# Fused adaLN attention and MLP block: V projected in eight tiles and shifted by DMA, K's last heads in the padding, head loads on one queue, a new instruction order

## The chip, the core and the metric

The kernel runs on one core of one Trainium2 chip. The core has five engines that each run a list of their own in order: TensorE (PE in the profile; PEld is its weight load), VectorE (DVE), ScalarE (ACT), GpSimd (POOL) and SyncE (SP); the lists meet at semaphores. DMAs are issued from SP's or ACT's list and are moved by 16 DMA engines. The metric is the time of one execution on the device in microseconds (us), lower is better.

## The reference

One transformer block for 2048 tokens of width 448, all in bf16: a vector c makes six modulation vectors; then a sliding, dilated attention (16 heads of 28, each token sees itself and 7 earlier tokens at stride 2) and an MLP of width 1792, each behind a modulated layer norm and added back through a gate.

```python
mod = (silu(c) @ w_mod).reshape(1, 6, 1, -1)
sa, ca, ga, sb, cb, gb = (mod[:, i] for i in range(6))
h = layernorm(x) * (1 + ca) + sa
...
idx = pos[:, None] - (arange(8) * 2)[None, :]          # keys of a token, masked where < 0
attn = softmax(where(mask, einsum('bhsd,bhswd->bhsw', q, k[idx]) * 28 ** -0.5, -1e9))
o = einsum('bhsw,bhswd->bhsd', attn, v[idx])
...
x = x + ga * (o @ wo)
h = layernorm(x) * (1 + cb) + sb
x = x + gb * (silu(h @ w1) @ w2)
```

## The kernel before

**Tokens.** The dilation of 2 splits the tokens by parity: even and odd tokens never meet, and in one parity (1024 steps) a token sees its last 8 steps. The projections run over NC = 4 chunks of 512 tokens (CP = 256 steps of both parities). Attention runs over NB = 9 blocks: a block takes 128 steps of keys and gives 112 or, for block 0, 128 queries (`q_of`, `nq_of`, lines 69 to 75); block b's keys begin at step 112 b.

**Norm.** `norm1` (line 595) normalises a chunk, transposes it (chunk 0 on PE, `on_pe`, line 520; the others by DMA transposes on SP, `on_dma`, line 545) and modulates it into `h1`, with the contraction of 448 split into three and a half tiles of 128. Since a block of keys reaches back over the chunk's edge, `h1` has 128 steps of room in front, and `halo` (line 611) copies 32, 64 or 96 steps of the chunk before into it.

**Projections.** `project` (line 615). Heads are padded from 28 to 32 rows (`pad`, line 562, into `wp` and `wp3`, whose columns 28 to 31 are zero), so that a matmul tile holds four heads: four tiles g = 0 to 3 a chunk, each of which makes Q and K of four heads with N = 512 columns (two halves of 256 in chunk 0). Each tile is a `duo` (line 569): 14 matmuls of 64 rows, run in pairs on the two halves of the array, in a first part of 6 and a second of 8, with a `turn` on POOL between them (line 308: a nop that orders the two halves' exchange of PSUM banks). An eviction on ACT or DVE follows (line 629). V is projected block by block (line 636): nine duos of 448 columns, one for each attention block, evicted into one of four buffers `vb` (line 640).

**Attention.** For a block and parity `logits` (line 655) makes 16 small matmuls into two PSUM banks, two exps on ACT (line 678), a mask product on DVE (line 704). `values` (line 716) makes 32 matmuls of probabilities and V (line 730), a normalisation on DVE (lines 735, 736) and a DMA transpose into `oT` (line 740). `out_proj` (line 746) takes 256 tokens: 14 matmuls with `wo`, which was multiplied by its gate on DVE (line 879) and copied half by half between partitions by two DMAs on SP (lines 882, 883), then two adds on DVE (line 768).

**MLP.** `ffn1` (line 782): norm, transposes on SP, 7 duos of 512 columns, silu on ACT (line 794). `ffn2` (line 799): 28 matmuls for 256 tokens, an add (line 823), a store on SP (line 826). The last 256 tokens go in two plain accumulations (line 832), then an add and a store each (lines 838, 841).

**Order.** Nothing here is scheduled at run time. Each operation is a numbered `P.op`, and `ORDER` (line 44) is the written list of all numbers; `emit` (line 215) issues them in that order, each on its engine ("v" or "a" after a number chooses DVE or ACT where both can). So each engine has a fixed list, and an instruction that waits holds all behind it. PSUM has NPS = 4 pairs of banks; the probabilities have 5 buffers, V has 4. `warm_up` (line 403) runs WARM = 8 matmuls on zeroes, then JUNK = 5 pairs more where the order puts them.

**Loads.** x's first 256 tokens are loaded on SP and the next 256 (`x0b`) and c on ACT's queue; all other loads are on SP in the order's sequence: w_mod's first two vectors, `wqk`, the other chunks of x, `wv`, and so on (lines 378 to 400).

If a softmax sum is out of range, a flag makes the program run a slower, safe version of itself; it isn't taken here.

Of the kernel before, what the change touches and what calls it, by code (L numbers as in the profile page):

```python
# [11 lines left out]
ACTF = mybir.ActivationFunctionType  # L12
# [3 lines left out]
D = 448  # L16
# [19 lines left out]
HW = 128 + CP  # L36
WARM, JUNK = 8, 5
# [74 lines left out]
def dram(ap, row, col, dims):  # L112

    w = ap.ap[0][0]
    return bass.AP(ap.tensor, ap.offset + row * w + col, [[r * w + c, n] for r, c, n in dims])

# [125 lines left out]
def layer(ctx, tc, io, safe):  # L242
# [19 lines left out]
    NV, NP, NX, NO, NH, NB2 = (4, 5, 2, 2, 3, 2) if not safe else (3, 3, 2, 1, 3, 1)  # L262
# [5 lines left out]
    wqk_t = ct([128, 2 * KT * HW], "wqk")  # L268
    wqk = wqk_t[:, 0:6 * D].rearrange("p (k n) -> p k n", k=3)
    wv = ct([128, KT, D], "wv")  # L270
    wqk3 = ct([128, D], "wqk3")
    wp = ct([128, 3, 2 * H, 32], "wp")
    wp3 = ct([128, H, 32], "wp3")
    wo = ct([128, 2, KT, D], "wo")
    w1 = ct([128, 3, F], "w1")
    w13 = ct([128, F // 2], "w13")
    w2 = ct([128, NF, D], "w2")
# [40 lines left out]
    for r, n in (("ps", NPS), ("v", NV), ("p", NP), ("xn", NX), ("o", NB2), ("out", NO), ("dma", 8)):  # L318
        P.resource(r, n)
# [679 lines left out]
```

## Time and profile before

| | us |
|---|---|
| median of three runs | 172.31 (170.99, 172.31, 172.62) |
| the profiled execution | 171.64 |
| its span | 169.9 |
| busy: PE, ACT, DVE, POOL | 162.0, 114.5, 96.1, 33.2 |
| F1 matmuls (line 791), F2 (lines 808, 832) | 44.7, 39.9 and 5.5 |
| QK matmuls (line 627) | 13.4, 7.0 and 6.7 by shape |
| V matmuls (line 638), out-projection (line 753) | 11.3 and 3.3, 13.0 |
| exps (line 678), silus (line 794) | 31.5, 27.3 |
| table loads on ACT (line 321) | 10.3 (8) |

The span is what the trace covers, from the first to the last event on the core. Busy times of matmuls count from the start of one to its modelled end, so they run over each other where matmuls are pipelined; the time that one costs PE is its distance to the next. In the lines below, "idle before" is time that the engine stood still just ahead of the instruction, and the name behind the arrow is what ended it. "SPq" and "ACTq" are DMA issues of these engines.

### The profile page before, as it was taken

Reading aid. Unit: us, or ns where it says so; the run is one execution under the profiler, and the core shown is the slowest. Engines: PE = TensorE matmul, PEld = TensorE weight load, DVE = VectorE, ACT = ScalarE, POOL = GpSimd, SP = SyncE. Lnnn points to the kernel's source line nnn. Section 1 sums busy time; section 2 is a strip of 40 time slices with the busy share of each in tenths; the row PEclk is TensorE's granted clock in tenths of the full one; section 3 lists DMA queues with packets and bytes.
Section 4 is the critical chain, followed back from the end, with each engine's and each line's share of the span. In section 5 each row is a group of like instructions: output and inputs, shape, how many; then the busy total and the mean of one; then the engine's idle time right before and its main releaser. Section 6 shows DMA issues by size and latency. Waiting matters only on the chain.

```text
span 169.9 us, 4812 instructions
## 1 busy us (share of the span) xinstructions
PE 162.0 (95%) x2015; PEld 83.9 (49%) x2015; DVE 96.1 (57%) x189; ACT 114.5 (67%) x163; POOL 33.2 (20%) x88
## 2 busy tenths in 40 slices
PE   7799999899999999999999999999999999999990
PEld 2258644545554564455644544655544444445450
DVE  4777999899979963895352577732473000000451
ACT  3148999999876889999878998662767862420000
POOL 7342424730502221132000205120150000000000
PEclk9959999999999999999999999999999999999999
DMA  4994448489979874022020030086008000000031
GB/s 142 289 326 165 99 94 314 78 202 242 176 185 252 177 198 106 0 66 46 20 54 0 4 90 22 2 112 178 6 10 224 0 4 0 0 4 0 38 136 64
DMA packets 32054, 17.51 MB, mean 103 GB/s; under 512 B 23896, under 2 KB 31640, under 8 KB 32024
## 3 DMA queue, kind: packets, MB, share of 16 engines
q1 hardware_dynamic: 31872, 16.90, 39.9%
q8 instruction: 17, 0.28, 0.7%
q10 hardware_dynamic: 152, 0.23, 0.5%
q14 instruction: 13, 0.11, 0.2%
HBM read 9.12 MB, written 1.84 MB: 64 GB/s over the span
## 4 chain that ended last, share of the span: by engine, by line
PE 75%; ACT 10%; DMA 6%; issue 3%; DVE 2%; POOL 1%; ACTq 0%; POOLq 0%
PE ps L791 25%; PE ps L808 22%; PE ps L627 7%; PE ps L753 6%; PE ps L638 5%; ACT p L678 4%; PE ps L730 4%; DMA wqk<-in_A_wqkv_dram 3%; PE ps L832 3%; PE ps L670 3%; DMA x_all<-in_A_x_dram 2%; ACT h L536 2%; ACT qk L630 1%; POOL rs L487 1%; ACT both L480 1%
## 5 line engine op out<-in xcount | busy, mean ns | idle before, releaser
L791 PE MATMUL ps<-h,w 64*128 64x512 bf16 x392 | 44.7, 376 | 0.0
L808 PE MATMUL ps<-w,both 64*128 64x448 bf16 x392 | 39.9, 349 | 0.0
L794 ACT ACTIVATE both<-ps 128x1024 bf16<-128x1024 f32 x28 | 27.3, 1023 | 13.9 <-PE ps L791 13.8
L678 ACT ACTIVATE p<-ps 128x896 bf16<-128x896 f32 (+1 forms) x36 | 31.5, 928 | 3.3 <-PE ps L670 3.2
L791 PEld LDWEIGHTS <-w 64*128 64x128 bf16 x392 | 19.5, 94 | 21.6
L808 PEld LDWEIGHTS <-both 64*128 64x128 bf16 x392 | 18.9, 94 | 17.7
L823 DVE TENSOR_TENSOR ot<-ps,x_all 128x896 bf16<-128x896 f32 x7 | 7.6, 1088 | 34.6 <-PE ps L808 34.3
L627 PE MATMUL ps<-h,wp 64*128 64x256 bf16 (+1 forms) x224 | 20.4, 323 | 0.6 <-ACT h L536 0.4
L627 PEld LDWEIGHTS <-wp 64*128 64x128 bf16 x280 | 13.9, 94 | 11.3 <-issue 1.1
L704 DVE TENSOR_TENSOR p<-p,maskb 128x1792 bf16<-128x1792 bf16 (+1 forms) x18 | 19.3, 1098 | 0.0
L768 DVE SCALAR_TENSOR_TENSOR x_all<-ps,x_all 128x448 bf16<-128x448 f32 x16 | 9.3, 618 | 9.7 <-PE ps L753 9.7
L487 POOL TENSOR_TENSOR rs<-rs,negh 128x2 f32<-128x2 f32 x16 | 13.8, 861 | 1.3
L753 PE MATMUL ps<-wo,oT 64*128 64x448 bf16 x112 | 13.0, 350 | 0.0
L480 ACT ACTIVATE wqk<-x_all,mv 128x448 bf16<-128x448 bf16 x16 | 10.7, 667 | 3.2 <-POOL mv L477 3.0
L477 POOL TENSOR_SCALAR mv<-sums 128x2 f32<-128x2 f32 x10 | 4.8, 479 | 40.0 <-DVE x_all L768 22.2
L638 PE MATMUL ps<-wv,h 64*128 64x448 bf16 x98 | 11.3, 350 | 0.2
L557 DVE TENSOR_SCALAR h<-h,modc 128x512 bf16<-128x512 bf16 x19 | 6.8, 408 | 6.6 <-DMA h<-xn 6.6
L630 ACT CAST qk<-ps 128x1024 bf16<-128x1024 f32 (+1 forms) x12 | 10.0, 871 | 0.7 <-PE ps L627 0.7
L321 ACT ACT_TABLE_LOAD x8 | 10.3, 1283 | 0.1
L486 POOL TENSOR_SCALAR rs<-mv 128x2 f32<-128x2 f32 x10 | 3.6, 356 | 33.3 <-ACT wqk L480 14.5
L736 DVE TENSOR_TENSOR o<-ps,rc 112x896 bf16<-112x896 f32 (+1 forms) x9 | 9.8, 1091 | 0.4
L501 DVE TENSOR_SCALAR xn<-x_all,mv,rs 128x512 bf16<-128x512 bf16 x23 | 8.8, 406 | 1.7 <-POOL rs L487 1.7
(84 smaller groups left out, 161.8 us busy)
## 6 DMA issues: line engine op xcount, KB each, us to landing
out_dram<-ot SPq DMA_DIRECT2D x7, 224.0 KB, 2.2
both<-in_w_mod_dram SPq DMA_DIRECT2D x2, 672.0 KB, 6.0
x_all<-in_A_x_dram SPq DMA_DIRECT2D x3, 448.0 KB, 7.0
w<-in_B_w_dram SPq DMA_DIRECT2D x3, 448.0 KB, 4.2
w<-in_B_w_dram SPq DMA_DIRECT2D x1, 896.0 KB, 5.3
both<-in_w_mod_dram SPq DMA_DIRECT2D x2, 336.0 KB, 5.8
w<-in_B_w_dram SPq DMA_DIRECT2D x1, 672.0 KB, 5.4
wqk<-in_A_wqkv_dram SPq DMA_DIRECT2D x1, 448.0 KB, 5.7
```

The source lines that it names most:

```text
L321: P.load = lambda t: S.preload_act_table(ACTF.Exp if t == "e" else ACTF.Silu)
L480: S.activation(out=scratch[late], in_=x_all[:, us[j], :], func=ACTF.Square, bias=mv[:, j, 0:1], accum_out=mv[:, j, 1:2])
L487: G.tensor_tensor(out=rs[:, j:j + n], in0=rs[:, j:j + n], in1=negh[:, 0:n], op=ALU.pow)
L627: return T.matmul(ps[:, j, 0:2 * n], lhsT=w.rearrange("p h d -> p (h d)"), rhs=h[rows, :, t, c0:c0 + n], start=start, stop=stop)
L630: copy_on(o)(out=qk[:, :, g, :, s0:s0 + n], in_=ps[:, :, 0:2 * n].rearrange("p j (t s) -> p j t s", t=2))
L638: return T.matmul(ps[:, j, 0:D], lhsT=h[rows, j, t, b0:b0 + 128], rhs=wv[rows, t, :], start=start, stop=stop)
L678: S.activation(out=out_, in_=ps[:, :, 0:4 * nq].rearrange("p j (g q) -> p j g q", q=nq), func=ACTF.Exp, scale=SCALE)
L704: V.tensor_tensor(out=p, in0=p, in1=maskb[:, 1 if b == 0 else 0, 0:nq].unsqueeze(1).to_broadcast([128, H, nq]), op=ALU.mult)
L753: return T.matmul(box["ps"][:, j, 0:D], lhsT=oT[rows, j, kk, s0:s0 + 128], rhs=wo[rows, j, kk, :], start=start, stop=stop)
L791: return T.matmul(ps[:, j, :], lhsT=w, rhs=h[rows, :, t, :], start=start, stop=stop)
L794: S.activation(out=hid[:, k % 2, :, i, :], in_=ps[:], func=ACTF.Silu)
L808: return T.matmul(box["ps"][:, par, 0:D], lhsT=hid[rows, k % 2, f % 2, f // 2, 128 * (2 * i + par):128 * (2 * i + par) + 128], rhs=w2[rows ...
```

## The change

1. **V once in eight tiles.** V is projected for the eight aligned tiles of 128 steps, two a chunk, into three buffers `va`. Blocks 0 and 8 coincide with tiles 0 and 7. For each of blocks 1 to 7 two DMAs inside SBUF copy the two parts of their 128 steps from two neighbouring tiles into one of three buffers `vb`. The halos and `h1`'s room for them go.
2. **Q and K in seven tiles.** In chunks 2 and 3 K's last four heads are computed in the padding: 4 heads of 28 columns are 112 columns, and seven tiles have 4 spare columns for each of 4 heads. Nine small copies on POOL (`fill`) put these weights there, after QK of chunk 0 and ahead of QK of chunk 1, from `wp` and three more small loads (`wx`). The fourth tile then makes only Q, 256 columns to a PSUM bank. Four DMAs a chunk (`move`) bring K's rows from the padding of the seven tiles to their place; block 4's logits need chunk 2's, block 6's need chunk 3's.
3. **Loads of the head.** w_mod's first vectors are loaded from ACT's queue; c and x0b on SP, x0b behind `wqk`. Later weight loads, V copies, moves and stores may be on either queue, as the order says.
4. **Another order**, with JUNK = 7.

```diff
-WARM, JUNK = 8, 5
+WARM, JUNK = 8, 7
...
-    NV, NP, NX, NO, NH, NB2 = (4, 5, 2, 2, 3, 2) if not safe else (3, 3, 2, 1, 3, 1)
+    NA, NV, NP, NX, NO, NH, NB2 = (3, 3, 5, 2, 2, 3, 2) if not safe else (3, 3, 3, 2, 1, 3, 1)
...
+    ld_ma = load_mod(0, 2 * D, [], ("act",))
+    tab = P.op(("act", 1290.0), lambda o: S.preload_act_table(ACTF.Silu), [ld_ma[1]["deps"][0]], name="table")
...
+    ld_x[0].append(load(224, after=[x["deps"][0] for x in [ld_qk[0][0], ld_qk[1][0], ld_qk[3][0]]], **first_x(1), run=1792, name="x0b"))
...
+    def fill(out_, m0, in_, t0, t1, deps, name="fill"):
+
+        to = out_[:, m0:m0 + 4 * (t1 - t0), DH:32].rearrange("p (t r) c -> p t r c", r=4)
+        return P.op(("pool", 300.0), lambda o: G.tensor_copy(out=to, in_=spread(in_, t0, t1)), deps, name=name)
...
+    def move(r, s0, n, deps):
+
+        return sp(680.0, lambda o: queue(o).dma_start(out=qk[32 * r:32 * r + DH, 1, 3, :, s0:s0 + n], in_=qk_t[32 * r + DH:32 * r + 32, 0:7, :, s0:s0 + n]), list(deps), 1700.0,
+                  kb=28.0, run=512, eng=EITHER, name="mv")[0]
...
-            for g in range(4):
+            for g in range(4 if k < 2 else 3):
...
+            if k > 1:
+
+                def make(ps, j, kk, rows, t, start, stop, c0=c0):
+                    w = wq3[rows, kk // 3] if j and kk in (1, 3) else wp[rows, kk, 12:16, :] if kk < 3 else wp3[rows, 12:16, :]
+                    return T.matmul(ps[:, j, 0:n], lhsT=w.rearrange("p h d -> p (h d)"), rhs=h[rows, :, t, c0 + n // 2 * j:c0 + n // 2 * j + n // 2], start=start, stop=stop)
...
+                done = done + [move(r, s0, n, done) for r in range(4)]
...
+        for t in (2 * k, 2 * k + 1):
+            def make(ps, j, kk, rows, kt, start, stop, t=t):
+                return T.matmul(ps[:, j, 0:D], lhsT=h[rows, j, kt, 128 * (t % 2):128 * (t % 2) + 128], rhs=wv[rows, kt, :], start=start, stop=stop)
...
+            def shifted(o, b, up):
+                r = 16 * b
+                to, way = (slice(r, 128), slice(0, 128 - r)) if up else (slice(0, r), slice(128 - r, 128))
+                queue(o).dma_start(out=v_of[b]()[to], in_=va_of[b - 1 + int(up)][way])
```

The numbers of the orders say little by themselves; in names, PE's list from the first QK to the first out-projection is (a and b are the two parts of a duo, Lb.p the logits of block b and parity p, AV the product with V, WO the out-projection):

```
before: QK0 first half | QK0 second half with L0.0 inside | L0.1 | V0 | V1a L1.0 V1b | QK1 (L1.1 inside) | AV0 |
        gate of wo | AV1 | L2.0 | V2 V3a L2.1 V3b | QK2 two tiles (L3.0 inside) | AV2 | WO0.0a L3.1 WO0.0b | ...
after:  junk | QK0 first half | transposes of its second half | gate of w2 | L0.0 | QK0 second half | L0.1 | V0 |
        L1.0 | gate of wo | V1a L1.1 V1b | QK1 | AV0 | V2a L2.0 V2b | second modulation | AV1 | V3a L2.1 V3b |
        QK2 two tiles (L3.0 inside) | AV2 | QK2 third tile (L3.1 inside) | WO0.0a | half tile | V5 | WO0.0b ...
```

Other lists, after: on SP, V2's copy for block 2 stands behind a load of w1; then a DMA transpose of chunk 3, one of `oT`, the first copy of `wo`, a V copy for block 3, the second copy of `wo`. On DVE the product of `wo` and its gate stands behind chunk 2's modulation and block 1's normalisation. One of chunk 2's four moves and one half of block 4's V copy are issued on ACT, the latter behind block 4's first exp pair. The ACT list has two changes between exp and silu tables fewer. In chunk 0 all four evictions of the first half are on ACT.

More of the change, by code (lines that the diff above doesn't have):

```diff
@@ L282, in layer @@
     h2 = [ct([128, 4, KT, 128], f"h2_{i}") for i in range(2)]
+    va = [ct([128, 2, H, 32], f"va{i}") for i in range(NA)]
     vb = [ct([128, 2, H, 32], f"v{i}") for i in range(NV)]
@@ L317, in layer @@
     P = Plan()
-    for r, n in (("ps", NPS), ("v", NV), ("p", NP), ("xn", NX), ("o", NB2), ("out", NO), ("dma", 8)):
+    for r, n in (("ps", NPS), ("va", NA), ("v", NV), ("p", NP), ("xn", NX), ("o", NB2), ("out", NO), ("dma", 8)):
         P.resource(r, n)
@@ L359, in layer, with sp, queue, load @@
         G.memset(t[:, D:D + 128], 0.0)
-    def sp(ns, fn, deps, land=0.0, give=(), kb=0.0, run=0, eng="sp", name="dma"):
-        a = P.op((eng, ns), fn, deps, take=("dma",), kb=kb, run=run, name=name)
+    def sp(ns, fn, deps, land=0.0, give=(), kb=0.0, run=0, eng=("sp",), name="dma"):
+        a = P.op([(e, ns) for e in eng], fn, deps, take=("dma",), kb=kb, run=run, name=name)
         return P.op(("none", land), none, [a], give=((a, "dma"),) + tuple(give), name=name + "'"), a
-    def load(kb, out, in_, after=(), run=896, q=None, name="ld"):
-        q = q or nc.sync
-        return sp(500.0, lambda o: q.dma_start(out=out, in_=in_), list(after), 2300.0 + kb / 0.36, kb=kb, run=run, eng="sp" if q is nc.sync else "act", name=name)[0]
+    EITHER = ("sp", "act") if not safe else ("sp",)
+    def queue(o):
+        return nc.scalar if o["eng"] == "act" else nc.sync
+    def load(kb, out, in_, after=(), run=896, q=("sp",), name="ld"):
+        return sp(500.0, lambda o: queue(o).dma_start(out=out, in_=in_), list(after), 2300.0 + kb / 0.36, kb=kb, run=run, eng=q, name=name)[0]
     def first_x(i):
@@ L596, in norm1 @@
         h = h1[k % NH]
-        after = [x for kk in (k - NH,) if kk >= 0 for x in qk_mm[kk] + v_mm[kk] + [halo[kk + 1]]] + (pads if k == 2 else [])
+        after = [x for kk in (k - NH,) if kk >= 0 for x in qk_mm[kk] + v_mm[kk]] + (pads + fills if k == 2 else [])
         if k == 0:
@@ L868, in ffn2 @@
             ad = P.op(("dve", 1007.0), lambda o, add=add: add(o), [prev], take=("out",), give=((first, "ps"),), name=f"add{u}")
-            before[:] = [ad, sp(400.0, lambda o, store=store: store(o), [ad], 1400.0, ((ad, "out"),), kb=224.0, run=1792, name=f"st{u}")[1]]
+            before[:] = [ad, sp(400.0, lambda o, store=store: store(o), [ad], 1400.0, ((ad, "out"),), kb=224.0, run=1792, eng=EITHER, name=f"st{u}")[1]]
     for k in range(NC):
@@ L880, in layer @@
                              [g_o] + ld_o, name="wo*g")]
[L881 to L883 removed]
+            wo_gated += [sp(500.0, f, wo_gated[0:1], 2400.0, kb=kb, run=896, eng=EITHER, name="wo'")[0] for f, kb in (
+                (lambda o: queue(o).dma_start(out=wo[half(1), 1, :, :], in_=wo[half(0), 0, :, :]), 224.0),
+                (lambda o: queue(o).dma_start(out=wo[half(0), 1, 1:4, :], in_=wo[half(1), 0, 0:3, :]), 168.0))]
             w2_gated = [P.op(("dve", 535.0), lambda o, f=f: V.tensor_tensor(out=w2[:, f:f + 2, :], in0=w2[:, f:f + 2, :],
```

125 lines of the change are left out of this document (76 added, 49 removed), and 44 rows, old and new, of the table ORDER.

## The prediction

> **What bounds the kernel now.** I read the page's table of engines, then the windows of 10 us (busy time of PE, weight loads, DVE, ACT, POOL, then the granted clock, the DMA share and GB/s), the groups of instructions, and the timeline and the chain where the change touches them.
>
> ```profile
> span 169.9 us, 4812 instructions
> PE 162.0 (95%) x2015; PEld 83.9 (49%) x2015; DVE 96.1 (57%) x189; ACT 114.5 (67%) x163; POOL 33.2 (20%) x88
> ...
> 20.00:30.00 10.00, 9.89 (x136) 4.75 (x132) 9.59 (x20) 9.94 (x19) 3.06 (x6) 1.00 0.67 196
> 30.00:40.00 10.00, 9.38 (x171) 4.96 (x168) 9.33 (x17) 9.82 (x16) 4.42 (x8) 1.00 0.78 167
> 40.00:50.00 10.00, 10.00 (x158) 5.55 (x154) 9.59 (x16) 8.42 (x13) 2.15 (x4) 1.00 0.99 187
> ...
> 12.73 1.59 PE L627 MATMUL ps<-h,wp 64*128 64x256 bf16 x26
> 18.05 1.02 ACT L678 ACTIVATE p<-ps 128x1024 bf16<-128x1024 f32 x1
> 34.01 0.37 PE L670 MATMUL ps<-qk 28*128 28x112 bf16 x14 [0.51 <-DVE o L736]
> 34.39 1.73 ACT L678 ACTIVATE p<-ps 128x896 bf16<-128x896 f32 x2 [0.15 <-PE ps L670]
> 165.99 0.02 issue
> ```
>
> Read it as three stages. Up to 12.73 us, when the first QK matmul runs, loads and the first norm set the time. From there to 34 us ACT is full (9.94 and 9.82 of 10), and PE is busy but often waits in its list. From 34.01, where block 2's logits resume, to 165.99 PE has no hole worth the name: 131.98 us in which each matmul taken out counts, and each new wait too, since PE runs a fixed list. The rest, 169.9 - 165.99 = 3.9 us, is the last add and store. In 30 to 50 us DVE (9.33 and 9.59 of 10) and the DMA engines (0.78 and 0.99) are close to full as well; the change's new copies go just there.
>
> **What it removes from PE.** The chain gives matmuls by start-to-start time:
>
> ```profile
> 44.04 1.30 PE ps L627 x12
> 45.92 1.73 PE ps L627 x16
> 51.72 0.76 PE ps L638 x8
> 56.53 0.57 PE ps L638 x6
> 47.65 0.90 PE ps L730 x32
> 61.80 0.78 PE ps L450 x4
> ```
>
> Two QK tiles of 512 columns are 28 matmuls in 1.30 + 1.73 = 3.03 us, 1.52 a tile. In chunks 2 and 3 the fourth tile shrinks to 256 columns and so to half, 0.76: 2 x 0.76 = 1.52 us less. A V block is 14 matmuls, 0.76 + 0.57 = 1.33 us, and eight remain of nine. PE loses 1.52 + 1.33 = 2.85 us, all after the 34.01 mark. The halo copies, one V eviction and half of two QK evictions leave DVE and ACT; I cost them at nothing, as PE ends last there.
>
> **What the new order moves.** Ahead of block 2's logits PE now also has the gate of w2 (0.78) and V2's first part (0.57), and no longer block 1's attn x V (0.90): 0.45 us more is done by then. So after that mark PE has 131.98 - 2.85 - 0.45 = 128.68 us. What counts is when the mark comes.
>
> **The head.** All but x's first load and w_mod queue on SP in the order wqk, x0b; w_mod starts at once on ACT's queue; seven junk pairs instead of five.
>
> ```profile
> 1.24 5.04 PE L405 MATMUL ps<-both 128*128 128x512 bf16 x12 [1.24 <-DVE both L339]
> 6.22 0.17 PE L417 MATMUL ps<-ident,both 4*128 4x4 bf16 x1
> 8.45 0.95 PE L433 MATMUL ps<-scT,both 128*128 128x1 bf16 x32
> 10.66 0.94 ACT L564 COPY wp<-wqk 128x896 bf16<-128x896 bf16 x1 [4.07 <-DMA wqk<-in_A_wqkv_dram]
> 12.45 0.63 DVE L470 BATCH_NORM_STATS2 st<-x_all 128x6 f32<-128x448 bf16 x1 [0.46 <-DMA x_all<-in_A_x_dram]
> 16.75 1.28 ACT L321 ACT_TABLE_LOAD   x1
> L630 ACT CAST qk<-ps 128x512 bf16<-128x512 f32 x4 | 2.3, 591 | 0.6 <-PE ps L627 0.6
> L630 ACT CAST qk<-ps 128x1024 bf16<-128x1024 f32 x8 | 7.8, 1011 | 0.2 <-PE ps L627 0.2
> L480 ACT ACTIVATE both<-x_all,mv 128x448 bf16<-128x448 bf16 x4 | 2.7, 680 | 0.0
> L453 ACT CAST gbc<-ps 128x448 bf16<-128x448 f32 x2 | 1.1, 540 | 0.0
> ```
>
> A junk matmul takes 5.04 / 12 = 0.42 us. PE's list is now: eight and two junk matmuls, c's transpose (6.2 as before), six junk to 8.7, the modulation's 32 matmuls to 9.7, two transposes to 10.4, six junk to 12.9, then QK. wqk waits for 224 KB less and lands some 0.7 us before 10.64, so pads and the first half's h are there by about 11.5: the junk, and not the loads, starts QK, at 12.9 instead of 12.73. x0b now lands last of the head, at about the 10.64 of wqk before, and its norm has x1's two statistics (not before 12.45) inside it on DVE: the second half's QK starts near 17 instead of 16.2. All four evictions of the first half are on ACT: the last matmul at 16.0, the last eviction at 17.0, the table load (1.28) to 18.3, so the first exp comes at 18.3, 0.25 late. The three small loads of K's last columns add some 1.6 us of issue to SP ahead of wv, which V needs only from 20 us on: nothing.
>
> From the first exp to block 2's exp before is 34.39 - 18.05 = 16.34 us of full ACT. In the new list this stretch has two more half evictions (2 x 0.59) and a square (0.68 and its read, 0.87), and one whole eviction (1.01) and a gate eviction (0.54) less: +0.5. Block 0's second logits now wait for those half evictions, an exposed round trip of some 0.4 (an estimate from the 34.01 to 34.39 of one logits and its exp). Block 2's exp: 18.3 + 16.34 + 0.5 + 0.4 = 35.5; its logits stand a square ahead of it: 34.7. **The mark comes 0.7 late.**
>
> **POOL's fills.** Nine copies into the padding, which QK1 waits for, behind QK0's last matmul (20.5). No row shows such a copy.
>
> ```profile
> 1.89 0.63 POOL L354 MEMSET v<- 128x128 bf16 x4
> 35.24 1.16 POOL L490 TENSOR_TENSOR nm<-mv,rs 128x2 f32<-128x2 f32 x1 [2.30 <-PE ps L638]
> 35.27 1.08 DVE L879 TENSOR_TENSOR wo<-wo,gbc 128x1792 bf16<-128x1792 bf16 x1
> ```
>
> A memset of 128 elements starts every 0.16 us; a tiny POOL operation that meets a long DVE product lasts as long as that, 1.16. Seven fills stand behind QK0: 1.1 to 8.1 us, beside 1.5 of POOL's own norm work, so done between 23 and 30. QK1 can't start before 27 for lack of banks. I take 0.3 each (nearest the memset, since DVE's masks come later in the list), hidden; the other end is 3 us.
>
> **Copies between tiles.** 14 V copies and 8 K moves, on SP or ACT. One row shows such a copy:
>
> ```profile
> wo<-wo SPq DMA_DIRECT2D x1, 224.0 KB, 5.3
> oT<-o SPq DMA_TRANSPOSE x9, 3.1
> 33.88 0.58 SPq L368 DMA_DIRECT2D w<-in_B_w_dram  x1
> 36.38 0.51 SPq L882 DMA_DIRECT2D wo<-wo  x1
> 36.93 0.59 SPq L883 DMA_DIRECT2D wo<-wo  x1
> 42.13 0.93 PE L753 MATMUL ps<-wo,oT 64*128 64x448 bf16 x8
> L736 DVE TENSOR_TENSOR o<-ps,rc 112x896 bf16<-112x896 f32 x8 | 8.7, 1091 | 0.3
> ```
>
> From issue to landing it took 3.1 (a transpose) to 5.3. I take 3.5, nearer the transpose, since a load of w2 was queued 2.5 us ahead of the 5.3 (33.88). A logits group is 0.37, an out-projection 1.33 like a V block. I lay the new lists along PE's clock from the mark at 34.7:
> - Block 2's attn x V is due after one logits, V2's rest 0.76, the second modulation 0.95, block 1's 0.90, V3 1.33, two more logits and two QK tiles: 8.1 later, 42.8. ACT ends V2's eviction at 35.5 + 1.73 + 1.01 = 38.2; its copy is issued on SP by 38.8 and lands 42.3 to 44.1: no wait, at worst 1.3.
> - Out-projection 0 is due 0.90 + 1.52 + 0.37 later, 45.6. The gated wo is now made on DVE behind chunk 2's modulation (its transposes land near 38.1, three steps of 0.41: 39.3) and block 1's normalisation (1.09 and a reciprocal: 40.8), and ends at 41.9. A V copy stands between wo's two copies: the second is issued by 43.5, 2.1 ahead of its use where it was 5.2 ahead (36.93 to 42.13), and lands 47.0 to 48.8. **Here I expect a wait: 1.4, at worst 3.2**; nothing if DVE runs that much earlier than I lay it.
> - K's moves are due for block 4's logits, two out-projections, three V blocks, two and a half QK tiles and a 0.90 later: 57. The last is issued on ACT near 52.2 and lands 55.7 to 57.5: nothing, at worst 0.5.
> - Block 4's V copy sits on ACT behind its first exp pair (57 + 0.4 + 1.73) and lands 63.1 to 64.9; the attn x V is due at 62.6: 0.5 to 2.3. The last w1 load has some 0.5 to spare.
>
> Of 1.4 + 0.5 I take 1.0, since during a wait DVE, ACT and the queues run ahead. DMA issues on ACT (ten of 0.4 to 0.6, by the 0.51 and 0.59 on SP) lie in ACT's idle time after 40 us (8.42 of 10 busy); if that is gone, one delays an exp by 0.6. Two table loads of 1.28 fewer pay for half of them. The stores change queue only: the tail stays 3.9, give or take 0.3.
>
> **Sum.** -2.85 - 0.45 + 0.7 + 1.0 = **-1.6 us**. The profiled execution took 171.64 (its span of 169.9 and 1.74 around it), so 170.0; the median of the three runs is 172.31, 0.67 above it: 170.7.
>
> **Rivals.**
> 1. No wait at all: copies land in 3.1, DVE is early, and banks freed sooner take back half of the head's 0.7. -2.85 - 0.45 + 0.35 = -2.95: 169.4. For it: the list of before, just as long, met no hole after 34 us. Against: wo's copies have lost 3 us of their lead.
> 2. The copies all take 5.3: 1.3 + 3.2 + 0.5 + 2.3 = 7.3, less some 1.0 that are shared: -2.6 + 6.3 = +3.7: 176.0, slower. For it: the DMA engines at 0.99 in 40 to 50 us, and 14 copies of V more to move there. Against: less load is queued ahead than at 33.88. It decides from about 4.8 us a landing, where the waits reach 4.3, the 2.6 gained and 1.7 beyond.
> 3. The half clock reaches QK:
>
> ```profile
> 7.00:8.00 1.00, 0.00 (x0) 0.00 (x0) 0.97 (x4) 0.00 (x0) 0.53 (x2) 1.00 1.04 289
> 10.00:11.00 1.00, 1.00 (x11) 0.79 (x9) 0.90 (x6) 0.34 (x1) 0.41 (x2) 0.50 0.86 294
> ```
>
> PE stood still in 7 to 8 us, and the granted clock was 0.50 in 10 to 11. The three junk pairs now fill that hole; but if w_mod, now sharing engines with x0a and wqk, lands after 8.7 + 1.2, the hole is back, later: six junk matmuls and QK0's first half (3 us) at half speed: +3 to the mark, -1.6 + 3.0 = +1.4: 173.7. The fills at their worst give the same +3. The Trainium skill, page "TensorE: Matmul & The Clock Gate", Part 1, lets the clock drop only after an idle window of about 3.4 us; by that neither hole would throttle and this rival would be out, at 170.7. The trace disagrees: about 1.3 us of standstill sufficed, so the rival stays. The Trainium skill, page "Trainium Kernel Development and Optimization", Key Constraints, says that DMAs from SP and ACT interleave on the same 16 engines; by that w_mod on its own queue gains only its place; no row here shows two full queues at once.
>
> **Chances.** Forecast 0.43 (169.9 to 171.6, nearly half of it below the line), no wait 0.22, slow copies 0.20, head late 0.15. About 1% is what a measurement of this kernel can tell from no change: 170.59 and 174.03. Faster is 0.20 of the forecast and the 0.22: 0.42; slower the slow copies and 0.04 of the late head: 0.24; the same 0.34. The range goes to 169.0, which leaves 0.07 below it, and to 174.9, which leaves 0.12 of the slow copies above.
>
> **What would show it.** PE's L627 group: 28 matmuls of 256 columns more and 28 of 512 fewer; L638's count 112 instead of 126; first QK near 12.9, block 2's logits near 34.7; a hole ahead of the first out-projection put down to wo's DMA and one ahead of block 4's attn x V. I am wrong if holes of over 1 us stand elsewhere after the mark, if POOL's fills end QK1's wait, if the granted clock is 0.5 once QK runs, or if PE's ideal saving isn't in the stretch from the mark to the last matmul.

## The result and the profile after

The changed kernel took 173.43 us (median of 20 runs, 172.42 to 179.34), the kernel before on the same chip 171.99 (20 runs, 170.89 to 173.07). The ratio is 1.0072, with an interval of 1.0045 to 1.0099: slower by 0.7%, inside the 1% that the prediction called no change. The forecast was 170.7, faster. Medians here are of all executions of a kernel and ratios of those within 1.5% of its fastest (15 of these 20 of the kernel after), so a ratio need not be the quotient of the medians.

The profiled execution of the kernel after is its fastest, 172.42 (span 170.7), against 171.64 (span 169.9): +0.78. The page of the kernel after, its first lines (compare the first two lines quoted of before):

```profile
span 170.7 us, 4836 instructions
...
PE 158.1 (93%) x2004; PEld 82.4 (48%) x2005; DVE 94.8 (56%) x190; ACT 109.5 (64%) x156; POOL 33.0 (19%) x96
```

PE is busy for 3.9 us less, and the span is longer: the work went and the time did not. Where it stayed is read by cutting the two spans at the same two events, the first matmul of block 2's logits (the prediction's mark) and the end of the last matmul. First the kernel before, then the kernel after, a window from the one event to the other (length; then busy time of PE, weight loads, DVE, ACT, POOL; granted clock, DMA share, GB/s):

```profile
34.01:165.99 131.98, 131.67 (x1618) 66.70 (x1617) 68.11 (x123) 90.20 (x124) 18.22 (x38) 1.00 0.36 82
```

```profile
33.07:165.82 132.75, 128.47 (x1630) 65.73 (x1628) 67.77 (x124) 85.06 (x117) 16.03 (x37) 1.00 0.39 89
```

| stage | before | after | difference | predicted |
|---|---|---|---|---|
| to the mark | 34.01 | 33.07 | -0.94 | +0.7 |
| mark to last matmul, PE busy | 131.67 | 128.47 | -3.20 | -3.30 |
| mark to last matmul, PE idle | 0.31 | 4.28 | +3.97 | +1.0 |
| last matmul to the span's end | 3.92 | 4.88 | +0.96 | 0 |
| span | 169.91 | 170.70 | +0.79 | -1.6 |

The saving is real; idle time in the middle eats it. The waits of PE in that stage, of the kernel after (what PE waited for, at which line, who ended it; us in total, times, longest):

```profile
PE ps L831 <- DMA oT<-o: 1.5, 1, 1.5
PE ps L673 <- POOLq L323: 1.3, 1, 1.3
PE ps L673 <- DVE o L812: 0.8, 1, 0.8
PE ps L453 <- DVE o L812: 0.4, 1, 0.4
PE ps L746 <- ACT p L754: 0.2, 1, 0.2
```

They sum to 4.2. In the same stretch before there is none; its last one, of 0.51, ends at the mark itself. None is one of the two waits that the prediction named (out-projection 0 for `wo`'s copies, block 4's attn x V for its V). In place, on PE's timeline of the kernel after (start, us, and in brackets the idle time ahead and what ended it):

```profile
33.07 0.37 PE L746 MATMUL ps<-qk 28*128 28x112 bf16 x16
...
34.71 0.94 PE L453 MATMUL ps<-scT,both 128*128 128x1 bf16 x32 [0.40 <-DVE o L812]
...
39.24 2.33 PE L673 MATMUL ps<-wqk,wp 64*128 64x512 bf16 x20 [0.79 <-DVE o L812]
41.51 0.38 PE L746 MATMUL ps<-qk 28*128 28x112 bf16 x16
43.15 1.04 PE L673 MATMUL ps<-wqk,wp 64*128 64x512 bf16 x8 [1.26 <-POOLq L323]
...
53.00 0.96 PE L806 MATMUL ps<-v,p 128*128 128x29 bf16 x32
...
60.49 0.93 PE L831 MATMUL ps<-wo,oT 64*128 64x448 bf16 x8 [1.55 <-DMA oT<-o]
```

Read them one at a time.
- **34.71 and 39.24: a PSUM bank.** The second modulation and QK2's first tile need banks that the normalisations of block 0 and block 1 still hold. On DVE block 0's stands behind an eviction of QK1 and two normalisation steps of chunk 3, block 1's behind a mask and three modulation steps of chunk 2. They end at 34.66 and 39.19 (line 812 in the DVE fence below).
- **43.15: POOL.** A QK tile's second part waits for its turn on POOL (line 323). That turn stands behind chunk 3's rstd, the reciprocal standard deviation of its norm (lines 506, 507). The two engines side by side, kernel after, POOL and then DVE:

```profile
29.73 0.19 POOL L506 TENSOR_SCALAR rs<-mv 128x2 f32<-128x2 f32 x1
30.01 0.71 POOL L507 TENSOR_TENSOR rs<-rs,negh 128x2 f32<-128x2 f32 x1
...
40.26 1.98 POOL L506 TENSOR_SCALAR rs<-mv 128x2 f32<-128x2 f32 x1 [6.43 <-PE ps L673]
42.33 0.71 POOL L507 TENSOR_TENSOR rs<-rs,negh 128x2 f32<-128x2 f32 x1
```

```profile
33.57 1.09 DVE L812 TENSOR_TENSOR o<-ps,rc 128x896 bf16<-128x896 f32 x1
...
38.10 1.09 DVE L812 TENSOR_TENSOR o<-ps,rc 112x896 bf16<-112x896 f32 x1
39.11 1.08 DVE L957 TENSOR_TENSOR wo<-wo,gbc 128x1792 bf16<-128x1792 bf16 x1
40.11 2.09 DVE L780 TENSOR_TENSOR p<-p,maskb 128x1792 bf16<-128x1792 bf16 x2
```

  The operation on two elements a partition that took 0.19 at 29.73 took 1.98: it began as DVE began two masks and ended as they did. PE stood behind it and the 0.71 that follows it from 41.9 to 43.15.
- **60.49: a transpose.** Block 3's attn x V starts at 53.00, its normalisation ends at 55.57, the transpose of its output is issued at 55.60, and PE goes on at 60.49, 4.9 later. The profile shows no landing for this one; those that it shows are 2.6 to 3.6, and before the change they were 2.6 to 6.6. PE had reached the out-projection at 58.94. Normalisation and issue, kernel after, then the landings of these transposes before the change:

```profile
54.48 1.09 DVE L812 TENSOR_TENSOR o<-ps,rc 112x896 bf16<-112x896 f32 x1
55.60 1.50 SPq L816 DMA_TRANSPOSE oT<-o  x1
```

```profile
DMA to landing us min/median/max: 2.6/3.1/6.6
```

### The profile page after: what moved, and what is told of

Same layout as the page of the kernel before. It is cut to its first block, busy times and chain, and to the rows that moved or that the text cites. A ratio compares the mean times of both kernels' runs of the same rounds, so it can differ in the third digit from the quotient of the medians.

```text
span 170.7 us, 4836 instructions
## 1 busy us (share of the span) xinstructions
PE 158.1 (93%) x2004; PEld 82.4 (48%) x2005; DVE 94.8 (56%) x190; ACT 109.5 (64%) x156; POOL 33.0 (19%) x96
## 4 chain that ended last, share of the span: by engine, by line
PE 61%; DMA 3%; ACT 1%; issue 1%; POOL 0%; DVE 0%; ACTq 0%
PE ps L869 25%; PE ps L886 22%; PE ps L831 4%; PE ps L910 3%; DMA oT<-o 3%; PE ps L806 3%; PE ps L746 2%; PE ps L673 1%; PE ps L695 1%; ACT p L754 1%; ACT wqk L500 0%; PE ps L684 0%; DVE ot L916 0%; POOL rs L507 0%; POOL rs L506 0%
## 5 line engine op out<-in xcount | busy, mean ns | idle before, releaser
L673 PE MATMUL ps<-h,wp 64*128 64x256 bf16 (+1 forms) x210 | 18.7, 319 | 0.7 <-DVE h L558 0.4
L673 PEld LDWEIGHTS <-wp 64*128 64x128 bf16 x252 | 12.5, 94 | 11.2 <-issue 2.1
L521 DVE TENSOR_SCALAR xn<-x_all,mv,rs 128x512 bf16<-128x512 bf16 x30 | 11.1, 406 | 8.2 <-POOL rs L507 8.2
L831 PE MATMUL ps<-wo,oT 64*128 64x448 bf16 x112 | 12.9, 350 | 1.5 <-DMA oT<-o 1.5
L507 POOL TENSOR_TENSOR rs<-rs,negh 128x2 f32<-128x2 f32 x16 | 11.5, 721 | 1.3
L676 ACT CAST qk<-ps 128x512 bf16<-128x512 f32 (+1 forms) x13 | 9.6, 786 | 2.5 <-PE ps L673 2.5
L575 ACT ACTIVATE h<-h,modc 128x512 bf16<-128x512 bf16 x9 | 6.9, 813 | 6.5 <-DMA h<-xn 6.5
L695 PE MATMUL ps<-wv,h 64*128 64x448 bf16 x84 | 10.0, 351 | 0.4 <-DVE va L699 0.3
L577 DVE TENSOR_SCALAR h<-h,modc 128x512 bf16<-128x512 bf16 x15 | 5.5, 407 | 7.6 <-DMA h<-xn 7.6
L806 PEld LDWEIGHTS <-p 128*128 128x128 bf16 x288 | 7.7, 96 | 2.4 <-issue 1.2
```

The source lines that it names most:

```text
L507: G.tensor_tensor(out=rs[:, j:j + n], in0=rs[:, j:j + n], in1=negh[:, 0:n], op=ALU.pow)
L521: V.tensor_scalar(out=out_, in0=in_, scalar1=mv[:, j, 0:1], scalar2=rs[:, j:j + 1], op0=ALU.subtract if b else ALU.add, op1=ALU.mult)
L673: return T.matmul(ps[:, j, 0:2 * n], lhsT=w.rearrange("p h d -> p (h d)"), rhs=h[rows, :, t, c0:c0 + n], start=start, stop=stop)
L695: return T.matmul(ps[:, j, 0:D], lhsT=h[rows, j, kt, 128 * (t % 2):128 * (t % 2) + 128], rhs=wv[rows, kt, :], start=start, stop=stop)
L806: T.matmul(box["ps"][:, par, h, 0:DH + 1], lhsT=p[:, at:at + 128], rhs=v[:, h, 0:DH + 1], start=True, stop=True)
L831: return T.matmul(box["ps"][:, j, 0:D], lhsT=oT[rows, j, kk, s0:s0 + 128], rhs=wo[rows, j, kk, :], start=start, stop=stop)
```

## The experiments

Each ratio is against the kernel before, run beside it on the same chip. The changed kernel's own is 1.0072.

**1. All four stores on SP again** (the tail: is it the queue?). In the order, the letter a is taken from four numbers:

```diff
-635a ... 623a ... 810a ... 817a
+635 ... 623 ... 810 ... 817
```

> The changed kernel with all stores of the output on SP's queue, in the same places of the order. Theory (the saving on PE is real; new waits of the new order and a longer tail took it back): last matmul near 165.8 as before this edit, the rest of the span 3.9 us instead of 4.85, so about 0.9 us faster than the changed kernel. Rival (extra DMA traffic between SBUF tiles slows everything): no change, the tail included, within 0.3 us.

Measured 173.99, ratio 1.0055 [1.0014, 1.0097]; last matmul to span's end 4.95, where 3.9 was expected. The queue is not the cause of the longer tail.

**2. Chunk 3's rstd ahead of the QK turn on POOL** (numbers 311 and 312):

```diff
-266 267 402 311 403 262 158 268 400 312 263
+266 311 312 267 402 403 262 158 268 400 263
```

> The changed kernel, with POOL's rstd and shift of tokens 14 and 15 of norm 1 put ahead of the turn of chunk 2's third QK tile instead of behind it. Theory: the 1.26 us in which PE waits for POOL inside chunk 2's second QK tile goes, and nothing takes its place at once: 1.0 to 1.3 us faster than the changed kernel, unless the next wait (out-projection 1.0 for its transposed input) grows by as much. Rival (DMA traffic): the POOL hole goes but the later DMA waits grow, under 0.4 us in all.

Measured 175.74, ratio 1.0089 [1.005, 1.0127]: no faster than the change. The wait on POOL grew to 2.2 instead of going. POOL in this kernel, then DVE beside it:

```profile
39.42 0.19 POOL L506 TENSOR_SCALAR rs<-mv 128x2 f32<-128x2 f32 x1 [4.11 <-ACT both L500]
39.70 4.33 POOL L507 TENSOR_TENSOR rs<-rs,negh 128x2 f32<-128x2 f32 x1
```

```profile
40.38 1.08 DVE L957 TENSOR_TENSOR wo<-wo,gbc 128x1792 bf16<-128x1792 bf16 x1
41.38 2.09 DVE L780 TENSOR_TENSOR p<-p,maskb 128x1792 bf16<-128x1792 bf16 x2
```

The first operation now slipped in ahead of DVE's product of `wo`, and the second, 0.71 elsewhere, ran for 4.33 beside the product of `wo` (40.38 to 41.46) and the two masks (to 43.47). My expectation had moved the operation without asking what DVE does 1 us later.

**3. Block 3's attn x V, its normalisation and its transpose earlier** in the order.

```diff
-288 261v 382 ... 279 422 323a ... 277 411 412 413 ... 455 423 282 ... 461 424 462 350 425 426 328 ... 464a 465 ... 437 57 58 295a
+288 422 261v 382 ... 279 323a ... 277 423 411 424 425 426 412 413 ... 455 282 ... 461 462 350 328 ... 464a 57 58 465 ... 437 295a
```

> The changed kernel with block 3's last mask, its product with V and its normalisation moved ahead of the second part of out-projection 0.1 and its two adds, the DMA transpose right behind them, and one load of w1 ahead of norm 2's transposes. Theory: the transposed input of out-projection 1.0 lands some 1.3 us earlier, so the 1.55 us wait there shrinks to about 0.3 and the time falls by about 1.2 us. Rival (DMA traffic makes that transpose take 4.85 us instead of the median 3.3): the landing stays late whatever its place, under 0.4 us gained.

Measured 173.43, ratio 1.01 [1.0067, 1.0133]. The wait for `oT` went, the one on POOL grew from 1.3 to 1.8, and two new ones stood in its place:

```profile
PE ps L673 <- POOLq L323: 1.8, 2, 1.3
PE ps L831 <- DVE qk L676: 1.7, 1, 1.7
PE ps L673 <- DVE o L812: 0.8, 1, 0.8
PE ps L831 <- DVE va L699: 0.7, 1, 0.7
```

DVE's earlier normalisation pushed its evictions back, and these hold banks as well. A wait taken away alone came back as another.

**4. No V copies.** Blocks 1 to 7 read the aligned tile instead of the shifted one; the 14 copies, and with them the shift, are left out.

```diff
-    NA, NV, NP, NX, NO, NH, NB2 = (3, 3, 5, 2, 2, 3, 2)
+    NA, NV, NP, NX, NO, NH, NB2 = (6, 1, 5, 2, 2, 3, 2)
```

> The changed kernel without the 14 V copies: blocks 1 to 7 read an unshifted V tile, from six V buffers; this part of the computation is left out, the rest is as it was. Theory: no wait of PE hangs on the copies, so the holes for POOL (1.26 us) and for a PSUM bank (0.8 and 0.4 us) stay; the wait for the transposed input of out-projection 1.0 may shrink by some tenths; in all 0 to 0.6 us faster. Rival (the 1.8 MB of copies slow transposes and loads): the DMA wait of 1.55 us goes, and the spread of the runs as well, 1.5 to 3 us faster.

Measured 172.96, ratio 1.0061 [1.0025, 1.0096] (171.73 to 173.96). The same four waits (POOL 1.3, `oT` 1.2, DVE 0.8 and 0.4): the copies aren't their cause.

**5. The fourth QK tile full again** in chunks 2 and 3, part 2 of the change undone in the same order, fills and moves included.

```diff
-        if k == 1:
+        if False:
...
-            for g in range(4 if k < 2 else 3):
+            for g in range(4):
...
-            if k > 1:
+            if False:
```

> The fourth QK tile of chunks 2 and 3 is whole again: no fills on POOL, no wx-built weights, no moves of K; V once per tile, the queues and the order stay those of the kernel after. Theory A (the two half tiles save PE time, and waits of the new order then eat it): PE's busy time rises by 1.5 us, the waits of PE after block 2's logits shrink by some of it, and the time is 0.3 to 1.5 us above the kernel after (its median 173.4). Rival B (fills and moves cost more than the half tiles save): the time falls by 0.5 us or more below the kernel after.

Measured 173.81, ratio 1.012 [1.0076, 1.0165]. The waits are those of the kernel after (1.3, 1.1, 0.7, 0.6). By the ratios the half tiles are worth 0.0048 x 172 = 0.8 us of their 1.5; the two intervals overlap, so it isn't shown that they gain anything, only that undoing them gains nothing and leaves the waits.

**6. Another order of everything**, DMA issues too: 31 of PE's 237 operations moved, 22 on DVE, 15 on ACT, 24 on POOL, 13 on SP, and others that changed from DVE to ACT, from ACT to DVE or from SP to ACT.

> The work, the engines' operations and the first 11 us are those of the kernel after; only the order on each engine between chunk 1's projection and the first second-layer products is another: POOL's small operations before the turns that they held up, normalisations of the attention blocks ahead of other vector work, transposes issued earlier. Theory A (the lost time is waits made by the order): PE's waits after block 2's logits fall from 4.3 us to 1.5 us or less, the end comes 2 to 4 us sooner, 168.5 to 171 us. Rival C (vector and scalar engines or the DMA landings bound this stretch, whatever the order): the holes move to other places with 3 us or more in all, and the time stays within 0.7 us of the kernel after's 172.4 to 174.

Measured 175.55, ratio 1.0221 [1.0183, 1.0259], and not what I expected. The V copies (issue to landing) in the kernel after and then here:

```profile
DMA to landing us min/median/max: 1.9/2.4/3.6
```

```profile
DMA to landing us min/median/max: 2.6/4.6/6.7
```

```profile
38.69 0.56 SPq L716 DMA_DIRECT2D v<-va  x1
```

```profile
45.45 0.95 PE L806 MATMUL ps<-v,p 128*128 128x29 bf16 x32 [2.30 <-issue]
```

The copy issued at 38.69 landed at 45.36, and block 2's attn x V started at 45.45 after 2.3 of standstill. Just ahead of it a load of an MLP weight (36.60) and a DMA transpose (37.29) were issued on SP, and the first copy of `wo` (38.34) on ACT; the weight had landed at 40.82. What held the copy up isn't shown. Then PE ran at half clock (this kernel's windows; the third figure from the end is the clock):

```profile
45.00:47.00 2.00, 1.55 (x40) 1.19 (x41) 0.45 (x2) 0.00 (x0) 0.00 (x0) 1.00 1.07 243
...
48.00:50.00 2.00, 2.00 (x16) 0.90 (x12) 0.99 (x1) 0.64 (x1) 0.00 (x0) 0.50 0.46 106
```

So the prediction's rival of slow copies is a mechanism that occurs, in this order and not in that of the change.

**7. The head with other junk**: two pairs of junk ahead of the transpose of c instead of one, none between it and the modulation instead of three.

```diff
-WARM, JUNK = 8, 7
+WARM, JUNK = 8, 5
```

> The kernel after with two junk pairs fewer: one pair stands ahead of c's transpose now, none between it and the first modulation columns; all else as it was. Theory D (the head's junk costs what its matmuls take, 1.5 us where they run warm and 2.1 to 2.7 where cold, and that is where executions of this kernel differ): the first QK matmul starts 0.4 us sooner than the 10.62 us of the kernel after where that was warm and 1.5 to 2 us sooner than the 12.2 to 12.5 us of the late heads; the median falls by 0.5 to 1.3 us. Rival E (the junk keeps the clock up): the granted clock falls to one half between 8 and 13 us and the time rises by 1 us or more.

Measured 172.17 (12 runs), ratio 0.9986 [0.9953, 1.0019]. Better than the change by about 0.9% of ratio, though its profiled execution had the half clock from 8 to 11 us and started QK at 11.35, where the profiled one of the change started it at 10.63.

**8. Experiments 6 and 7 together.**

> The order of e6_other_order and the head of e7_head_without_junk together. Theories A and D: their gains add, 168 to 170.5 us, under the kernel before's 171.6 to 172. Rivals C or E: 172 us or more.

Measured 176.68, ratio 1.0145 [1.0069, 1.0222], where a gain was expected. Block 2's attn x V waits for its copy again, 3.2: experiment 6's loss stays.

**9 and 10. Five and nine moves by hand**, on the head of experiment 7: chunk 3's rstd one turn later on POOL, block 0's `oT` earlier on SP, one product of w2 and its gate behind block 3's normalisation, chunk 2's two transposes exchanged; in 10 also a norm ahead of a mask, V6's first part and block 3's attn x V ahead of a QK tile, one modulation on ACT.

> The kernel after with the head of e7_head_without_junk and five moves in the order, no load and no copy of V moved: the first of the two transposes of chunk 2's normalised rows ahead of the second one on SP (its rows are ready 4 us sooner); the two POOL operations of chunk 3's last statistics behind the turn of QK2.0.1 that they held up; the transpose of block 0's output ahead of chunk 2's V copies and of a w1 load on SP; a gating of w2 behind block 3's normalisation on VectorE. Theory A (the lost time is these waits): PE's waits for POOL's queue (1.26 us) and for the normalisations ahead of QK2 (0.79 us) go and the one for block 3's output shrinks (1.55 to 1.0 us), the time falls by 1.5 to 2.5 us against e7's 172.17, to 169.7 to 170.7. Rival C (the landings of DMAs or the vector engines bound the stretch): other waits take their place and the time stays at 171.5 to 172.7.

> e9_five_moves and four more: the product with V of block 3 and the first half of V6 ahead of QK3's first tile on PE, a normalisation ahead of block 1's second mask and a modulation of chunk 3 on ScalarE instead of VectorE. Theory A: the wait for block 3's output shrinks to 0.5 us or less, 0.3 to 0.6 us under e9. Rival C: no better than e9, since a wait for a vector operation takes its place, as in e3_av3_early.

Measured 173.53, ratio 1.0089 [1.0048, 1.013], and 172.43, ratio 1.0012 [0.9971, 1.0053]. Experiment 9 was expected at 169.7 to 170.7. The wait on POOL is gone in both, and others stand elsewhere: in 9 for two of DVE's evictions (1.0, 0.6) and ACT's `h` (0.5), in 10 for ACT's `h` (1.3; experiment 7 has that one too) and still for `oT` (0.8).

**11. The order changed as a whole on PE, DVE, ACT and POOL**, with the DMA issues in the sequence of experiment 9 and its head: 22, 23, 21 and 20 operations moved, and 11 more changed between DVE and ACT. On POOL, in names (T is a turn; mean, rstd and nm are steps of a norm's statistics, each for two tiles of 128 tokens, with the number of the first):

```
after:  T V1 | rstd12 | mean10 | T QK1 | T QK1 | nm8 | T QK1 | rstd10 | T QK1 | mean14 | nm10 | T V2 | nm12 | T V3 |
        T QK2 | rstd14 nm14 | T QK2 ...
here:   mean10 | T V1 | fills | nm8 | T QK1 | T QK1 | rstd10 nm10 rstd12 | T QK1 | T QK1 | nm12 mean14 | T V2 |
        rstd14 nm14 | T V3 | T QK2 | T QK2 ...
```

> The head of e7 and an order between block 0's products and the first second-layer products that is changed in many places on PE, VectorE, ScalarE and POOL, with every DMA issue in the sequence of e9. Theory A: all waits of PE after block 2's logits together under 1.5 us, 168 to 169.7 us. Rival C, or V copies and transposes that land later than before the moves, as in e6_other_order: 171 us or more.

Measured 170.36, ratio 0.9929 [0.9899, 0.996] (168 to 169.7 was expected): faster than the kernel before, and than experiment 9 (1.0089), which has the same head and the same sequence of DMA issues. Waits after the mark: 0.4 for `oT` and 0.2 for an exp.

**12. One DMA less** in experiment 11: the two small loads of `wx`'s last half tiles are one.

```diff
-load(14, wx[half(0), 2, :], ...), load(14, wx[half(1), 2, :], ...)
+load(28, wx[:, 2, :], pairs_of(A_wqkv, 128, D - 112, 256, 2 * D - 112, 112), late, run=224, name="wx")
```

> e11_many_moves with two 14 KB loads of the head merged into one, so that the program issues one DMA less and the last store stands elsewhere in the list of DMA semaphores that SP reads off at the end. Theory F (the longer tail of the kernel after is that list: its last store has the first of eight semaphores, and seven reads of 0.07 to 0.09 us each come after it, where in the kernel before they went by while the store was under way): at most two reads follow the landing of the last store, and from the last matmul's end to the end of the span it takes 4.0 to 4.3 us instead of 4.64; the time falls by 0.3 to 0.7 us, to 169.7 to 170.1. Rival G (the last store itself lands later, for whatever reason): 4.5 us or more as before, no gain.

Measured 169.84, ratio 0.989 [0.9858, 0.9922]. At its end the kernel reads eight DMA semaphores on SP one after the other. The reads of the kernel before, the kernel after and experiment 12 (first and last start):

```profile
L966 SPq EVENT_SEMAPHORE  x8: 17/17/17, 167.2 to 168.5; - x8
```

```profile
L1044 SPq EVENT_SEMAPHORE  x8: 17/17/17, 168.8 to 169.3; - x8
```

```profile
L1044 SPq EVENT_SEMAPHORE  x8: 17/17/17, 164.6 to 165.9; - x8
```

The last stores are issued at 166.66, 166.50 and 163.70. Before, seven reads went by while the store was under way; after, the first read waited for the store, and seven more followed, 0.5 us. That fits DMAs that take the eight semaphores in turn: one DMA less moves the last store from the first semaphore read to the last. Last matmul to span's end: 4.64 in experiment 11, 4.24 here. The intervals of the two ratios overlap, so the gain is read from the traces.

**13. One junk pair more** ahead of the transpose of c, on experiment 12.

```diff
-WARM, JUNK = 8, 5
+WARM, JUNK = 8, 6
```

> e12_tail_one_dma_less with one junk pair more ahead of c's transpose, 14 matmuls there instead of 12. Theory H (the half clock of 8 to 11.6 us, seen in some executions, comes of the standstill of about 1 us ahead of c's transpose): the granted clock stays at 1.0 and QK starts near 9.9 us instead of 11.1 to 11.4; the median falls by 0.3 to 1 us. Rival: c's transpose is held up by up to 0.5 us and the clock falls all the same; no gain or 0.2 to 0.5 us lost.

Measured 169.33 (169.20 to 169.44), ratio 0.9863 [0.9836, 0.989]: faster than the kernel before by 1.4%. Against experiment 12 the spread is what changed: there five of six executions lie between 169.10 and 170.09, one at 172.29. Its waits after the mark, then the window from the mark to the last matmul:

```profile
PE ps L746 <- ACT va L699: 0.2, 1, 0.2
PE ps L746 <- ACT p L754: 0.2, 1, 0.2
```

```profile
34.02:163.36 129.34, 128.32 (x1599) 65.15 (x1596) 65.54 (x123) 84.69 (x115) 13.30 (x35) 1.00 0.39 88
```

In this order the second modulation (33.13 to 34.02, 0.89) stands ahead of the mark and not behind it. With it the stretch is 130.23, where the prediction had 129.68 (128.68 and 1.0 of waits) and the kernel after 132.75. Some of the idle time moved ahead of the mark: from the first QK matmul (9.94 here, 10.63 in the kernel after) to the last matmul it is 153.42 here and 155.19 there, 1.77 less.

**14. Block 2 unmasked** in the change's own order: the two masks that stand beside POOL's rstd are left out, so block 2's attention isn't masked.

```diff
+            if b != 2:
-            V.tensor_tensor(out=p, in0=p, in1=maskb ...
+                V.tensor_tensor(out=p, in0=p, in1=maskb ...
```

> The kernel after without the mask of block 2's two halves: that multiplication is left out, so VectorE is idle or at other work when POOL comes to the statistics of chunk 3 at about 40 us. Theory A' (VectorE's masks keep POOL's small operations from running): the first of them takes 0.2 us instead of 1.98, and PE's wait for POOL's queue of 1.26 us goes. Rival: the operation is slow for another reason and still takes over 1 us.

One run, 173.09. POOL in this kernel:

```profile
40.76 0.19 POOL L506 TENSOR_SCALAR rs<-mv 128x2 f32<-128x2 f32 x1 [6.77 <-PE ps L673]
```

0.19 where it was 1.98, and PE's wait on POOL is gone: the masks on DVE held POOL, and POOL held PE. The Trainium skill, page "SBUF — State Buffer", section "Who interferes with whom", says that a DVE instruction with two inputs in SBUF contends with a GpSimd instruction that reads SBUF, and that whichever comes first has the shared ports until it is done while the other stands still. The runs agree that the two contend: 0.19 or 1.98 for the first of a pair of tiny operations, 0.71 or 4.33 for the second, by what DVE ran beside them. They don't bear out that the first one wins, as far as the profile's rough spans on POOL tell: at 35.24 before the change and at 39.70 in experiment 2 the POOL operation began 0.03 and 0.68 ahead of the DVE product, and was the one that stood still. The time did not follow: a new wait of 1.0 for a DVE eviction stands ahead of an out-projection, and the waits still sum to 4.4.

## Why the prediction was wrong

**Right: what leaves PE.** 2.85 saved and 0.45 moved ahead of the mark, 3.30 together; PE's busy time after the mark fell by 3.20. POOL's fills took 0.19 to 0.37 each (0.3 was taken) and ended at 23.87, ahead of QK1 at 25.36, which did not wait for them. The V copies landed in 1.9 to 3.6, where the profile shows a landing, and none was waited for.

**The step that failed: "Of 1.4 + 0.5 I take 1.0".** PE's idle time after the mark rose by 3.97, and by the prediction's own sign, holes of over 1 us elsewhere (1.26 and 1.55), its mechanism was wrong. The step laid one kind of event along PE's list, the landing of DMAs, and asked only where a copy would be late. It left out three others that the trace of before had rows for:
- POOL's list as a place where PE waits. The row of 1.16 for a tiny POOL operation beside a long DVE product stood in the prediction, and was used for the fills alone. The turns of QK and V stand in the same list; behind the rstd of chunk 3 one cost 1.3. Experiment 14 shows the cause (in one execution), experiment 2 the size it can take.
- DVE as the holder of banks. The row of 34.01 stood in the prediction with 0.51 of just such a wait. Normalisations end later as more stands ahead of them on DVE, and PE can't start the next tile: 0.8 and 0.4.
- The lead of the transposes of attention. Block 3's attn x V stood 8.0 us ahead of its out-projection before and 5.9 after, if the wait is taken off; normalisation and transpose needed 2.6 and 4.9. A transpose of 4.9 lies within the range of before; the lead no longer covered it.

The two waits that were named didn't come: `wo`'s copies and block 4's V landed in time. That 173.43 lies inside the forecast's range of 169.0 to 174.9 is luck as far as the profiled execution shows: the part above 171.6 stood for slow copies and a late head, and it had neither.

**The order, not the parts.** Experiments 1 to 4 leave the four waits or exchange them, experiment 5 takes a part of the change away and keeps the waits, and experiments 2, 3, 9, 10 and 14 change one or a few places and get other waits. Experiments 11 and 13 keep all parts, change the order as a whole, and have 0.6 and 0.4 of waits; from experiment 9 to 11, with one head and one sequence of DMA issues, the ratio falls from 1.0089 to 0.9929. So the change's own order gives back its gain. Not all of the loss is there: two junk pairs less, with the rest of the order kept, bring 1.0072 to 0.9986. The parts were not tried one by one in the order of before.

**The head: "the junk, and not the loads, starts QK, at 12.9".** QK started at 10.63 and the mark came 0.94 early instead of 0.7 late; of the 2.27 that QK gained on the forecast 1.64 reached the mark. The price of a junk matmul, 0.42, was taken from twelve that ran at the start of the kernel before; those later in the list ran in half that. The kernel after:

```profile
1.24 4.45 PE L425 MATMUL ps<-both 128*128 128x512 bf16 x10 [1.24 <-DVE both L350]
...
6.68 1.47 PE L425 MATMUL ps<-both 128*128 128x512 bf16 x6
7.99 0.94 PE L453 MATMUL ps<-scT,both 128*128 128x1 bf16 x32
...
9.45 1.24 PE L425 MATMUL ps<-both 128*128 128x512 bf16 x5
10.63 0.52 PE L673 MATMUL ps<-h,wp 64*128 64x256 bf16 x4
```

4.45 / 10 = 0.45 at first; later six take 7.99 - 6.68 = 1.31 from the first start to the next operation, 0.22 each. The Trainium skill, page "TensorE: Matmul & The Clock Gate", Part 1, gives 427 ns cold and 216 ns warm for a matmul of 512 columns; the trace agrees, and I should have read 0.42 as the price of a cold PE alone. The -0.94 also compares two states of the head: the profiled execution of before had a granted clock of 0.50 from 10 to 12 us, that of after 1.00.

**The half clock** was a rival, in its place: six junk matmuls and QK0 late. In some executions it is there. The profiled one of experiment 2, which has the head of the change unaltered:

```profile
6.95 0.17 PE L437 MATMUL ps<-ident,both 4*128 4x4 bf16 x1 [1.89 <-ACT both L438]
...
12.30 1.91 PE L673 MATMUL ps<-h,wp 64*128 64x256 bf16 x26
```

```profile
8.00:9.00 1.00, 1.00 (x4) 0.31 (x3) 0.11 (x1) 0.70 (x1) 0.00 (x0) 0.50 0.89 283
```

The clock is 0.50 where the kernel after has 1.00, QK starts at 12.30 and the mark falls at 34.57. Experiment 5 is like it (0.50 in 8 to 10 us, QK at 12.24, the mark at 34.62). In experiment 4 QK starts at 12.29 and the mark falls at 34.73 as well, but the column of the clock reads 1.00 all along, and only the six junk matmuls show the low speed, 2.54 us where the kernel after has 1.31:

```profile
6.88 2.74 PE L423 MATMUL ps<-both 128*128 128x512 bf16 x6
...
8.00:9.00 1.00, 1.00 (x4) 0.31 (x3) 0.00 (x0) 0.67 (x1) 0.00 (x0) 1.00 0.93 271
```

So a late head is shown in three executions, and its mark near the 34.7 that was forecast for another reason. Why the head is late in some executions stays open. That the median of the kernel after lies 1.0 above its profiled execution, and that of before 0.35, fits such executions; that they make up the whole of it isn't shown, since the median's own profile isn't there.

**The tail: "stays 3.9, give or take 0.3".** It rose by 0.96: 0.53 for seven reads of semaphores behind the last store, and 0.44 for a store that took 2.30 from issue to the read that it frees instead of 1.86. Experiment 1 rules out the queue, experiment 12 shows the reads.

In sum: the profiled execution was forecast at 170.0 and took 172.42, 2.4 more: 3.07 in the stretch after the mark and 0.96 in the tail, less 1.64 in the head. What the median has beyond that, 0.3, isn't traced.

The changes that followed, by their ratios to the kernel before: 1.0072 as changed, 0.9986 with less junk, 0.9929 with another order, 0.989 with one DMA less, 0.9863 with one junk pair more.

## What to carry to other kernels

When one engine runs a fixed list and is the bound, work taken out of it is a gain only if every other list still delivers in time: lay all of them along its clock, the tiny operations and turns of POOL and whoever frees its buffers among them, not the transfers alone. A hole mended by itself tends to open the next one, so judge an order by the sum of waits in the stage and not by the wait that went. Price an instruction from a row in the same state of its engine: here a junk matmul cost 0.45 at the start and 0.22 later.

## What the runs showed of the hardware

- A tiny POOL operation beside DVE products with both inputs in SBUF stood still for the whole chain of them: 0.19 alone, 1.98 beside two masks, and another 4.33 instead of 0.71 beside three products.
- A hole of 1.9 us at the start, or 2.3 in the middle, was followed by half clock within 2 us. Holes of about 1 us ahead of c's transpose went both ways: 0.88 (experiment 11) and 1.30 (experiment 7) with half clock behind them, 1.23 (experiment 1) and 1.38 (experiment 14) without. Cold speed (0.45 a junk matmul) shows at the start, and in experiment 4 up to 9.4 us, while the column of the granted clock reads 1.00. With two more junk matmuls ahead (14 in all) six runs lay within 0.24 us; with 12, five of six lay within 0.99 and one 2.2 above them.
- Copies of V inside SBUF landed in 1.9 to 3.6 us in the order of the change and in 2.6 to 6.7 in experiment 6. PE was let go 4.9 us after the issue of one DMA transpose; before the change such transposes landed in 2.6 to 6.6, 3.1 in the median. What makes some of them slow stays open.
- Where the last store stands among the eight DMA semaphores that SP reads at the end made 0.4 to 0.5 us: seven reads behind it took 0.53, and the tail fell by 0.40 when they came ahead of it.
